# Linear attention feeding a sine-gated MLP on one core: one weight quarter loaded ahead of another, and the second chunk's query turns and scores placed anew

## The chip, the cores and the metric

The kernel runs on one core of a Trainium2 chip. Five engines work side by side: TensorE (PE; its weight loads are shown as PEld), VectorE (DVE), ScalarE (ACT), GpSimd (POOL) and SyncE (SP). Each takes its own instructions strictly in order and waits for others through semaphores. The metric is the device time of one execution in microseconds, as the median of several runs.

## What is computed

The reference has two parts. The first is block-wise linear attention over q, k, v of shape 4 x 8 x 768 x 64 (batch, heads, positions, width) with a decay `lam` for each head, in blocks of 64 positions; the second takes the attention output as 3072 tokens of 512 numbers and runs a two-layer MLP with the "snake" activation.

```python
for b in range(nb):                       # nb = 768 / 64 blocks
    intra = (qb @ kb.T * Dmask) @ vb      # scores inside the block, masked by powers of lam
    inter = (qb * lam_pow) @ kv_state     # what earlier blocks left
    out[:, :, sl] = intra + inter
    kv_state = lam_block * kv_state + (kb * rev_pow).T @ vb
x = out as (3072, 512)
h = x @ w_in                              # 512 -> 2048
g = h + sin(alpha * h)**2 / alpha
y = g @ w_out                             # 2048 -> 512
```

## The kernel before

The 768 positions are cut into six **chunks** of 128 positions (t = 0 to 5), each over all 4 batches and 8 heads, so a chunk is 512 tokens. For each chunk the MLP runs in a **stage** g. Its first layer is `hidden(g, f)` for f = 0 to 15: four matmuls of 128x128 by 128x512 into one PSUM bank (L507), a sine on ACT (L510), a square on ACT (L515) or, for some f of stage 0 (f = 3, 5, 7, 9, 13), on DVE (L523), and then `finish(g, f)` on DVE (L524), which makes the 512 columns of `gall` from both. Its second layer is cut into 16 **units** (m, part): `project(g, m, part)` is four matmuls (L535) that add a quarter of the 2048 hidden features for 128 tokens into a bank; part p reads `w_out_sb[p]`, the p-th quarter of `w_out`. `w_in_sb[i]` is a quarter of `w_in`, needed by f = 4i to 4i + 3.

The order is written out by hand: the schedule is manual, and each engine runs its instructions in the order in which the program states them. Units of stage g wait in a list and `run(n)` takes the next n of them; they are placed between the other work of PE.

Attention of chunk t + 1 is placed within stage t. It is done in two **pairs** of batches, pr 0 (batches 0, 1) and pr 1 (batches 2, 3), in these steps:

- `turn`, `turns_pair`: PE transposes k or q (L320, L338, L340, L341) into a PSUM bank, and ACT or DVE copies them out (L344, L324).
- `scores`: 32 small matmuls of 64x64 (L443) from the turned k and q into two banks; `masks` multiplies them by the decay table on DVE (L450).
- `states`: 32 matmuls of 64x64 (L423); `update` folds them into the running state on DVE (L399, or L403 in four pieces) and casts it on POOL (L392).
- `outputs_first`: 31 matmuls of 64x64 (L457) of queries with the cast states; it ends with a tiny ACT copy (L472) of two turned columns, for which the first matmul of `outputs` waits. `outputs`: one more L457 and 32 matmuls (L482) of masked scores with v. `leave` scales the result on DVE (L489) into `xt`, the input of the next stage's first layer.

Chunk 0 has a form of its own; chunk 1, the second, is placed by hand in the last third of stage 0, from `hidden(0, 10)` on, and between stages 0 and 1. All of the change but the order of two loads is there.

Loads of k, q, v and of the weights are issued by POOL, each a DMA with a cast from fp32 to bf16; the order of issue is the order of the program. The last loads before the first stage are `load_w_in(0)` in two pieces, then 1, 2, 3, and later in the text, with no other instruction of POOL between, `load_w_out(0)`. Behind it POOL makes `kdec` of chunk 0 (L257) and then issues k, q, v of chunk 1.

PSUM has eight banks. `H0` gives the bank of each `hidden(0, f)`. Those that matter here: the turned k and, in the version after, the turned q of pair 1 of chunk 1 use bank 4; `states` and `scores` are given their two banks in the call.

Of the kernel before, what the change touches and what calls it, by code (L numbers as in the profile page):

```python
# [15 lines left out]
def kernel(  # L16
# [41 lines left out]
    def bank(nm, n, dtype=FP32):  # L58
        return psum.tile([P, 512 if dtype is FP32 else 1024], dtype, name=nm, tag=f"b{n}")
# [27 lines left out]
    def load_w_in(i, w0=0, w1=512):  # L87
        w = slice(512 * i + w0, 512 * i + w1)
        nc.gpsimd.dma_start(out=w_in_sb[i][:, :, w0:w1], in_=moe_w_in[:, w].rearrange("(c p) g -> p c g", p=P))  # L89

    def load_w_out(i):
        nc.gpsimd.dma_start(out=w_out_sb[i][:],
                            in_=moe_w_out[i * 512:(i + 1) * 512, :].rearrange("(f p) d -> p f d", p=P))

    def load(t, nm, b0, b1):
        dst, src = NAT[nm]
        to = dst[t][:, b0:b1, :, :].rearrange("p b h e -> p (b h) e")
        by_head = src[b0:b1, :, t * T:(t + 1) * T, :].rearrange("b h p e -> p (b h) e")
        n = H * (b1 - b0)
        if t > 1 and nm != "v" and b0 == 2:  # L100
            nc.gpsimd.dma_start(out=to[:, 0:n - 1, :], in_=by_head[:, 1:n, :])
            nc.gpsimd.dma_start(out=to[:, n - 1:n, :], in_=by_head[:, 0:1, :])
        else:
            nc.gpsimd.dma_start(out=to, in_=by_head)  # L104
# [20 lines left out]
        nc.gpsimd.dma_start(out=vn[0][:, 3, hs, :], in_=v[3, hs, 0:T, :].rearrange("h p e -> p h e"))  # L125
    load_w_in(0, 0, 2 * P)
    load_w_in(0, 2 * P, 512)
    for i in range(1, 4):
        load_w_in(i)

    fill = consts.tile([P, 512], BF16, name="fill")
    nc.vector.memset(fill[:], 1.0)  # L132
# [3 lines left out]
    def spin(n, bk, cols=256):  # L136
        ps = bank("hps", bk)
        for _ in range(n):
            nc.tensor.matmul(out=ps[:, 0:cols], lhsT=fill[:, 0:P], rhs=fill[:, 0:cols], start=True, stop=True)  # L139
# [82 lines left out]
    V, G, A = nc.vector, nc.gpsimd, nc.scalar  # L222
# [4 lines left out]
    def turned_by_one(t, pr):  # L227
        return bool(t) and pr == 1

    def in_turn(t, pr):  # L230
        return t > 1 and pr == 1

    def where(t, pr, n):
        if turned_by_one(t, pr):
            n = (n - 1) % (2 * H)
        return n % 2, n // 2
# [89 lines left out]
    def halves(hd):  # L326
        return slice(hd * D, (hd + 1) * D)

    def turns_pair(t, nm, b, bk, engines):
        src, n = (kn, 0) if nm == "k" else (qn, 1)  # L330
        ps = bank("T_ps", bk, BF16)[:].rearrange("p (u c i) -> p u c i", u=2, c=HP)
        flat = src[t][:, b:b + 2].rearrange("p b h d -> p (b h) d")
        o = int(turned_by_one(t, b // 2) and not in_turn(t, b // 2))
        for u in range(2):
            for hp in range(HP):
                h = u * H + 2 * hp + o
                if h + 2 <= 2 * H:
                    nc.tensor.transpose(out=ps[:, u, hp, :], in_=flat[:, h:h + 2, :], identity=iden[:])  # L338
                else:
                    nc.tensor.transpose(out=ps[LO, u, hp, :], in_=flat[:, h, :], identity=iden[:])  # L340
                    nc.tensor.transpose(out=ps[HI, u, hp, :], in_=flat[:, 0, :], identity=iden[:])  # L341
        for u, eng in enumerate(engines):
            if eng is nc.scalar:
                eng.copy(out=both[t][:, n, b + u, :, :], in_=ps[:, u])  # L344
            else:
                eng.tensor_copy(out=both[t][:, n, b + u, :, :], in_=ps[:, u])
# [25 lines left out]
    def head(tile, t, pr, n):  # L372
        s = (n - 1) % (2 * H) if in_turn(t, pr) else n
        return tile[t][:, 2 * pr + s // H, s % H, :]
# [12 lines left out]
    def decay_state(n, pr):  # L387
        nc.gpsimd.tensor_tensor(out=pair(SD, pr), in0=pair(S_of[n], pr), op=ALU.mult,  # L388
                                in1=L64[:, pr].unsqueeze(1).unsqueeze(3).broadcast_to([P, 2, HP, D]))

    def cast_state(n, pr, dst):
        nc.gpsimd.tensor_copy(out=pair(dst, pr), in_=pair(S_of[n], pr))  # L392
# [18 lines left out]
    def banks_of(kind, t, prs, ns, nm):  # L411
        ns = ns or [AB[2 * pr + n] for pr in prs for n in range(2)]
        for k, n in enumerate(ns):
            att[kind, t, prs[k // 2], k % 2] = bank(nm, n)[:].rearrange("p (u c i) -> p u c i", u=2, c=HP)

    def states(t, prs=BOTH, ns=None):
        banks_of("KV", t, prs, ns, "KV_ps")
        for pr in prs:
            for h0 in range(0, 2 * H, 2):
                for blk in range(2 if t < NT - 1 else 1):  # L420
                    for h in (h0, h0 + 1):
                        half, m = where(t, pr, h)
                        nc.tensor.matmul(out=att["KV", t, pr, blk][halves(half), m // HP, m % HP, :],  # L423
                                         lhsT=head(kdec, t, pr, h)[halves(blk)],
                                         rhs=vn[t][halves(blk), 2 * pr + h // H, h % H, :], start=True, stop=True)
# [9 lines left out]
    def scores(t, prs=BOTH, ns=None):  # L435
        banks_of("F", t, prs, ns, "F_ps")
        for pr in prs:
            for u in range(2):
                for hp in range(HP):
                    for blk in range(2):  # L440
                        for hd in range(2):
                            w = halves(blk)
                            nc.tensor.matmul(out=att["F", t, pr, hd][w, u, hp, :],  # L443
                                             lhsT=KT[t][halves(hd), 2 * pr + u, hp, w],
                                             rhs=QT[t][halves(hd), 2 * pr + u, hp, w], start=True, stop=True)
# [8 lines left out]
    def inter(t, pr, half, m, blk, start):  # L454
        n = (2 * m + half + turned_by_one(t, pr)) % (2 * H)
        u, h = n // H, n % H
        nc.tensor.matmul(out=att["O", t, pr, blk][halves(h % 2), u, h // 2, :],  # L457
                         lhsT=home(t, blk)[halves(half), 2 * pr + m // HP, m % HP, :],
                         rhs=QT[t][halves(half), 2 * pr + m // HP, m % HP, halves(blk)],
                         start=start, stop=False, skip_group_check=True)  # L460

    def outputs_first(t, prs=BOTH, ns=None):
        banks_of("O", t, prs, ns, "O_ps")
        begun = set()
        order = [(pr, half, m, blk) for m in range(2 * HP) for blk in range(2) for pr in prs for half in range(2)]
        for blk in range(2):
            order.remove((prs[0], 0, 0, blk))
        for pr, half, m, blk in order + [(prs[0], 0, 0, 1)]:
            inter(t, pr, half, m, blk, (pr, half, blk) not in begun)
            begun.add((pr, half, blk))  # L470
        seen = QT[t][LO, 2 * prs[0], 0, 0:T:D]
        nc.scalar.copy(out=seen, in_=seen)  # L472
# [145 lines left out]
    outs(0, 3, 4, None, 1)  # L618
    nc.vector.reciprocal(out=r_sb[:], in_=alpha_sb[:])
    spin(3, 3)  # L620
    load_w_out(0)
    decay_k(0, 0, 2)
    decay_k(0, 2, 4)
    mask_table()
# [25 lines left out]
    def run(n):  # L650
        for _ in range(min(n, len(behind))):
            behind.pop(0)()
# [3 lines left out]
    for f in range(NFC):  # L656
        hidden(0, f)
        if f in (1, 10):
            states1(0, f // 10, 2 if f == 10 else 4)
        if f == 10:  # L660
            decay_k(1, 0, 2)
            decay_state(1, 0)
            cast_state(1, 0, home(1, 0))
            load(1, "q", 2, 4)
            load_w_out(2)
            load_w_out(3)
            load(2, "v", 0, 2)
        if f in (11, 12):
            run(1)
        if f == 12:  # L670
            turns_pair(1, "k", 0, 4, (A, A))
        if f == 13:
            turn(1, "q", 0, 2, V)
            turn(1, "q", 1, 3, V)
        if f == 14:
            scores(1, (0,), (4, 2))
            masks(1, 0)
        if f == 15:
            run(1)
            states(1, (0,), (4, 2))  # L680
            finish(0, 14)
            update(1, 0, 0)
        if f != 14:
            finish(0, f)
# [1 line left out]
    decay_state(1, 1)  # L686
    cast_state(1, 1, home(1, 0))
    update(1, 1, 0)
    run(2)
    turns_pair(1, "k", 2, 4, (A, A))  # L690
    run(1)
    outputs_first(1, (0,), (5, 0))
    load(2, "v", 2, 4)
    run(1)
    outputs(1, (0,))
    leave(1, 0)
    states(1, (1,), (4, 2))
    update(1, 0, 1)
    run(1)
    turns_pair(1, "q", 2, 5, (A, A))  # L700
    load(2, "k", 0, 2)
    run(1)
    update(1, 1, 1)
    scores(1, (1,), (5, 0))
    masks(1, 1)
    load(2, "k", 2, 4)
    outputs_first(1, (1,), (4, 2))
    load(2, "q", 0, 2)
    load(2, "q", 2, 4)
    run(2)  # L710
    outputs(1, (1,))
    leave(1, 1)
    run(2)
# [100 lines left out]
```

## Time and profile before

| what | value |
|---|---|
| median of 3 runs | 207.41 us (207.37 to 207.46) |
| the profiled execution's own time | 207.33 us |
| its span, first to last instruction | 205.6 us |
| time around the span | 1.7 us |
| granted TensorE clock, mean | 0.999 |
| PE busy | 198.1 us (96%) |
| DVE, ACT, POOL busy | 131.5, 143.2, 106.5 us (64%, 70%, 52%) |
| L507, first-layer matmuls | 94.3 us |
| L535, second-layer matmuls | 90.4 us |

In a timeline row the columns are: start and length in us from the span's start, engine, line, operation, what it writes and reads with its shape, how many instructions were merged into the row, and in square brackets how long the engine sat idle before it and what ended that. A row of PE gives 1.04 us for four matmuls of 512 columns, yet the next row starts 0.86 us after it: matmuls are pipelined, so the pace is read from start to start. Some matmul records are missing in a trace (a row says x3 where four ran), and then the start of the row is late.

### The profile page before, as it was taken

What the parts mean: (1) busy time and instruction counts of PE and PEld (TensorE: products, weight loads), DVE (VectorE), ACT (ScalarE), POOL (GpSimd) and SP (SyncE); (2) the same over time, 40 slices, a digit from 0 to 9 for tenths busy, and PEclk for the clock granted to TensorE, in tenths of its full rate; (3) what the DMA queues carried; (4) which work ended last, traced back from release to release, by engine and by line L of the source; (5) the groups of instructions that cost most, each with busy time, mean ns of one, the idle gap of its engine ahead of it and who ended that gap; (6) DMA issues with size and microseconds to landing.
All of it is one profiled execution on the core that took longest, in us unless ns stands there. A gap on an engine that the chain in (4) does not pass through costs nothing.

```text
span 205.6 us, 5385 instructions
## 1 busy us (share of the span) xinstructions
PE 198.1 (96%) x2235; PEld 98.3 (48%) x2265; DVE 131.5 (64%) x219; ACT 143.2 (70%) x241; POOL 106.5 (52%) x112
## 2 busy tenths in 40 slices
PE   7999989999999999999999999999999999999994
PEld 2764445554454444445444445444445444444443
DVE  7794979473889878967556967555967544444000
ACT  7798987224999799676776666776666787887121
POOL 8999939988979975999966930002000000000000
PEclk9999999999999999999999999999999999999999
DMA  8999999999989999899999929401101101110213
GB/s 132 170 178 205 203 162 176 189 176 154 150 275 105 128 151 184 82 150 155 152 149 155 181 64 192 117 3 51 54 0 54 51 0 54 53 51 0 104 51 105
DMA packets 96683, 24.49 MB, mean 119 GB/s; under 512 B 87938, under 2 KB 94226, under 8 KB 96658
## 3 DMA queue, kind: packets, MB, share of 16 engines
q0 software_dynamic: 74528, 13.37, 86.9%
q1 hardware_dynamic: 22128, 10.76, 25.5%
q8 instruction: 18, 0.29, 0.6%
q14 instruction: 7, 0.06, 0.1%
q10 hardware_dynamic: 2, 0.00, 0.0%
HBM read 27.27 MB, written 6.29 MB: 163 GB/s over the span
## 4 chain that ended last, share of the span: by engine, by line
PE 84%; DMA 7%; POOL 6%; issue 1%; ACT 1%; POOLq 0%; ACTq 0%
PE ops L535 39%; PE hps L507 35%; DMA w_out<-in_moe_w_out_dram 7%; PE O_ps L457 2%; POOL w_in L89 2%; PE hps L560 2%; PE F_ps L443 2%; PE KV_ps L423 2%; POOL kn L104 1%; PE O_ps L482 1%; POOL vn L104 1%; PE T_ps L338 1%; POOL qn L114 1%; POOL vn L125 1%; ACT QKT L344 1%
## 5 line engine op out<-in xcount | busy, mean ns | idle before, releaser
L524 DVE SCALAR_TENSOR_TENSOR gall<-s,r_sb,hps 128x512 bf16<-128x512 bf16 x96 | 71.1, 745 | 44.5 <-ACT s L515 44.3
L507 PE MATMUL hps<-xt,w_in 128*128 128x512 bf16 x369 | 94.3, 379 | 1.1 <-issue 0.3
L535 PE MATMUL ops<-w_out,gall 128*128 128x512 bf16 x353 | 90.4, 380 | 1.7 <-DMA w_out<-in_moe_w_out_dram 0.6
L510 ACT ACTIVATE s_sb<-hps,alpha_sb 128x512 bf16<-128x512 f32 x96 | 65.2, 684 | 32.0 <-PE hps L507 31.5
L515 ACT ACTIVATE s<-s_sb 128x512 bf16<-128x512 bf16 x91 | 57.3, 630 | 2.8
L507 PEld LDWEIGHTS <-w_in 128*128 128x128 bf16 x384 | 36.6, 98 | 42.8 <-DMA w_in<-in_moe_w_in_dram 0.3
L535 PEld LDWEIGHTS <-gall 128*128 128x128 bf16 x368 | 34.6, 98 | 41.5 <-DMA w_out<-in_moe_w_out_dram 1.1
L257 POOL TENSOR_TENSOR kdec<-kn,R 128x1024 bf16<-128x1024 bf16 x12 | 22.9, 1937 | 4.2 <-DMA kn<-in_k_dram 4.1
L392 POOL CAST sb<-S 128x512 bf16<-128x512 f32 x20 | 12.3, 621 | 21.3 <-DVE S L399 21.3
L388 POOL TENSOR_TENSOR SD<-S,L 128x512 f32<-128x512 f32 x16 | 16.8, 1050 | 8.6 <-DVE S L399 8.5
L489 DVE TENSOR_TENSOR xt<-O_ps,Etab 128x512 bf16<-128x512 f32 x20 | 12.8, 684 | 6.4 <-PE O_ps L482 6.4
L104 POOL DMA_DIRECT2D vn<-in_v_dram x13 | 14.7, 1137 | 0.0
L542 DVE COPY o_sb<-ops 128x512 f32<-128x512 f32 x15 | 10.3, 689 | 4.2 <-PE ops L535 4.2
L450 DVE TENSOR_TENSOR STm<-F_ps,C 128x512 bf16<-128x512 f32 x20 | 12.8, 683 | 0.3 <-PE F_ps L443 0.3
L544 ACT COPY o_sb<-ops 128x512 f32<-128x512 f32 x8 | 4.6, 576 | 12.0 <-PE ops L535 12.0
L399 DVE TENSOR_TENSOR S<-SD,KV_ps 128x512 f32<-128x512 f32 x16 | 10.8, 683 | 0.1
L104 POOL DMA_DIRECT2D kn<-in_k_dram x9 | 10.0, 1113 | 0.4 <-issue 0.3
L344 ACT COPY QKT<-T_ps 128x512 bf16<-128x512 bf16 x8 | 4.3, 586 | 5.3 <-PE T_ps L341 5.3
L139 PE MATMUL hps<-fill 128*128 128x256 bf16 (+1 forms) x24 | 6.5, 391 | 1.4 <-DVE fill L132 1.4
L104 POOL DMA_DIRECT2D qn<-in_q_dram x6 | 7.1, 1188 | 0.0
L457 PEld LDWEIGHTS <-sb 64*64 64x64 bf16 x320 | 4.3, 108 | 4.8 <-issue 4.7
L356 DVE TENSOR_TENSOR STm<-F_ps,C 128x512 bf16<-128x512 f32 x8 | 5.2, 686 | 0.8 <-PE F_ps L352 0.4
(92 smaller groups left out, 116.8 us busy)
## 6 DMA issues: line engine op xcount, KB each, us to landing
out_dram<-o_sb SPq DMA_DIRECT2D x19, 256.0 KB, 2.4
vn<-in_v_dram POOLq DMA_DIRECT2D x10, 256.0 KB, 7.9
w_out<-in_moe_w_out_dram POOLq DMA_DIRECT2D x4, 512.0 KB, 10.8
w_in<-in_moe_w_in_dram POOLq DMA_DIRECT2D x3, 512.0 KB, 9.4
kn<-in_k_dram POOLq DMA_DIRECT2D x6, 256.0 KB, 8.7
qn<-in_q_dram POOLq DMA_DIRECT2D x6, 256.0 KB, 8.5
out_dram<-o_sb SPq DMA_DIRECT2D x8, 128.0 KB, 1.8
kn<-in_k_dram POOLq DMA_DIRECT2D x4, 240.0 KB, 6.7
```

Source lines behind the costliest of these rows:

```text
L104: nc.gpsimd.dma_start(out=to, in_=by_head)
L257: nc.gpsimd.tensor_tensor(out=kdec[t][:, b0:b1, :, :], in0=kn[t][:, b0:b1, :, :], in1=R[:, o:o + H].unsqueeze(1).unsqueeze(3).broadcast_to ...
L388: nc.gpsimd.tensor_tensor(out=pair(SD, pr), in0=pair(S_of[n], pr), op=ALU.mult, in1=L64[:, pr].unsqueeze(1).unsqueeze(3).broadcast_to([P, ...
L392: nc.gpsimd.tensor_copy(out=pair(dst, pr), in_=pair(S_of[n], pr))
L399: nc.vector.tensor_tensor(out=S, in0=pair(SD, pr), in1=ps, op=ALU.add)
L450: nc.vector.tensor_tensor(out=st[:, hd], in0=att["F", t, pr, hd], op=ALU.mult, in1=of_mask(C64, t, pr, hd).unsqueeze(1).broadcast_to([P, 2 ...
L489: nc.vector.tensor_tensor(out=xview(t)[:, 2 * pr:2 * pr + 2, blk, :, :], in0=att["O", t, pr, blk], in1=Eb, op=ALU.mult)
L507: nc.tensor.matmul(out=hps[:], lhsT=w[:, c, (f % 4) * P:(f % 4 + 1) * P], rhs=xt[g][:, c, :], start=(c == 0), stop=(c == NDC - 1))
L510: nc.scalar.activation(out=s_sb[:], in_=hps[:], func=ACTF.Sin, scale=alpha_sb[:, f:f + 1])
L515: nc.scalar.activation(out=s2[:], in_=s_sb[:], func=ACTF.Square)
L524: nc.vector.scalar_tensor_tensor(out=gall[g][:, f, :], in0=s2[:], scalar=r_sb[:, f:f + 1], in1=hps[:], op0=ALU.mult, op1=ALU.add)
L535: nc.tensor.matmul(out=ops[:], lhsT=gall[g][:, f, m * P:(m + 1) * P], rhs=w_out_sb[part][:, f % 4, :], start=(f == 0), stop=(f == NFC - 1))
```

## The change

Three edits. First, `load_w_out(0)` is moved from behind the set-up of chunk 0 to between `load_w_in(2)` and `load_w_in(3)`. As no other POOL instruction stands between the two places, the order of POOL's issues changes by a swap of these two loads alone.

Second, in stage 0 the turns of q of pair 0 move from f = 13 to f = 14, and `scores` and `masks` of pair 0 from f = 14 to f = 15. On PE `hidden(0, 14)` now stands before the turns of q and `hidden(0, 15)` before the scores. On DVE the two copies of the turned q (L324) stand behind the square and the `finish` of f = 13, where they stood ahead of them.

Third, behind stage 0: three units instead of two run before the turns of k of pair 1, and none between these turns and `outputs_first` of pair 0. The turns of q of pair 1 move ahead of `states` of pair 1, into bank 4 instead of 5. `states` of pair 1 writes banks 2 and 4 instead of 4 and 2, and `scores` of pair 1 follows it at once; the two units that stood between `states` and `outputs_first` stand now between `scores` and `outputs_first`, one unit runs between the turns of q and `states`, and one instead of two between `outputs_first` and `outputs` of pair 1. No instruction is added or removed on any engine; the number of units run up to the start of stage 1 is the same (the line numbers of the changed kernel are two higher behind the first edit, one of them taken back at the second).

```diff
     load_w_in(0, 2 * P, 512)
-    for i in range(1, 4):
-        load_w_in(i)
+    load_w_in(1)
+    load_w_in(2)
+    load_w_out(0)
+    load_w_in(3)
...
     spin(3, 3)
-    load_w_out(0)
     decay_k(0, 0, 2)
...
         if f == 12:
             turns_pair(1, "k", 0, 4, (A, A))
-        if f == 13:
+        if f == 14:
             turn(1, "q", 0, 2, V)
             turn(1, "q", 1, 3, V)
-        if f == 14:
+        if f == 15:
             scores(1, (0,), (4, 2))
             masks(1, 0)
-        if f == 15:
             run(1)
             states(1, (0,), (4, 2))
             finish(0, 14)
...
     update(1, 1, 0)
-    run(2)
+    run(3)
     turns_pair(1, "k", 2, 4, (A, A))
-    run(1)
     outputs_first(1, (0,), (5, 0))
     load(2, "v", 2, 4)
     run(1)
     outputs(1, (0,))
     leave(1, 0)
-    states(1, (1,), (4, 2))
+    turns_pair(1, "q", 2, 4, (A, A))
+    run(1)
+    states(1, (1,), (2, 4))
     update(1, 0, 1)
-    run(1)
-    turns_pair(1, "q", 2, 5, (A, A))
     load(2, "k", 0, 2)
+    scores(1, (1,), (5, 0))
     run(1)
     update(1, 1, 1)
-    scores(1, (1,), (5, 0))
     masks(1, 1)
     load(2, "k", 2, 4)
+    run(1)
     outputs_first(1, (1,), (4, 2))
     load(2, "q", 0, 2)
     load(2, "q", 2, 4)
-    run(2)
+    run(1)
     outputs(1, (1,))
```

## The prediction

> **What bounds the kernel now.** I read the page first: TensorE is busy nearly throughout and nearly all of the chain that ended last is TensorE's, with one foreign piece of size, a weight load.
>
> ```profile
> span 205.6 us, 5385 instructions
> PE 198.1 (96%) x2235; PEld 98.3 (48%) x2265; DVE 131.5 (64%) x219; ACT 143.2 (70%) x241; POOL 106.5 (52%) x112
> PE 84%; DMA 7%; POOL 6%; issue 1%; ACT 1%; POOLq 0%; ACTq 0%
> ```
>
> Next I asked for TensorE's waits from 48 us to the end. One group is left:
>
> ```profile
> PE hps L507 <- issue: 0.3, 2, 0.2
> ```
>
> From stage 1 on TensorE waits for nobody, so what the change is worth is the shift of the first matmul of stage 1, `hidden(1, 0)`, and the rest of the program follows it. The timeline of TensorE has the stretch where the second chunk is placed in stage 0:
>
> ```profile
> 25.61 1.04 PE L507 MATMUL hps<-xt,w_in 128*128 128x512 bf16 x4
> 27.28 1.04 PE L535 MATMUL ops<-w_out,gall 128*128 128x512 bf16 x4 [0.63 <-DMA w_out<-in_moe_w_out_dram]
> 28.15 1.03 PE L507 MATMUL hps<-xt,w_in 128*128 128x512 bf16 x4
> ...
> 29.88 0.61 PE L338 MATMUL T_ps<-iden,kn 128*128 128x128 bf16 x8
> 30.33 1.03 PE L507 MATMUL hps<-xt,w_in 128*128 128x512 bf16 x3
> 31.19 0.61 PE L320 MATMUL T_ps<-iden,qn 128*128 128x128 bf16 x8
> 31.64 1.03 PE L507 MATMUL hps<-xt,w_in 128*128 128x512 bf16 x4
> 32.59 0.45 PE L443 MATMUL F_ps<-QKT 64*64 64x64 bf16 x32
> 32.97 0.82 PE L507 MATMUL hps<-xt,w_in 128*128 128x512 bf16 x3
> 33.84 1.03 PE L535 MATMUL ops<-w_out,gall 128*128 128x512 bf16 x4
> ```
>
> From start to start, four wide matmuls take 0.865 us (28.15 to 29.88 is two groups), a set of eight turns 0.45 us (29.88 to 30.33), four wide ones ahead of a 64x64 set 0.95 us (31.64 to 32.59), the set itself 0.38 us. `hidden(0, 11)` starts at 25.61, so its successor, unit (0, 0), could start at 26.47; it starts at 27.28. The wait is 0.81 us, for `w_out`'s first quarter.
>
> **Edit 1, the two loads.** The loads' rows:
>
> ```profile
> 13.50 13.73 DMA w_out<-in_moe_w_out_dram
> L89 POOL DMA_DIRECT2D w_in<-in_moe_w_in_dram x5: 812/826/842, 9.8 to 12.8; - x5
> DMA to landing us min/median/max: 5.2/7.6/11.2
> ```
>
> The fifth and last `w_in` piece is issued at 12.8 and lands, being the slowest, after 11.2 us, at 24.0. `w_out` lands at 13.50 + 13.73 = 27.23, the next in line. The two have the same size and adjacent issues, so I let them trade places: `w_out` lands near 24.0 and unit (0, 0) runs at 26.47, which gains 0.81. `w_in`'s last quarter is first read by `hidden(0, 12)`, at 26.47 + 0.865 = 27.34; if it lands at 27.23, it is in time by 0.1. The last place took 3.2 us, from 24.0 to 27.2. If that length goes with the place or with the load, the sum of both is the same and 27.23 stands. If the load behind `w_out`'s is slow and `w_out` as well, `w_in` lands 0.6 later at about 27.85 (the piece before lands at 12.0 + 9.4, 2.6 ahead of 24.0, by the same view). I take 27.23.
>
> The turns of k then run at 27.34 + 1.73 = 29.07. Their k had landed when POOL's `kdec` started on it:
>
> ```profile
> 28.95 1.90 POOL L257 TENSOR_TENSOR kdec<-kn,R 128x1024 bf16<-128x1024 bf16 x1 [3.16 <-DMA kn<-in_k_dram]
> ```
>
> So they come through with 0.1 to spare, for the loads behind the swapped pair keep their places.
>
> **Edit 2, turns of q and scores one f later.** Laid out by the steps above: `hidden(0, 13)` 29.52, `hidden(0, 14)` 30.38, turns of q 31.24 (their q was there by 31.19 in the version before), `hidden(0, 15)` 31.69, scores 32.64, unit (2, 0) 33.02. That is 0.82 ahead of 33.84, if the scores find their q. ACT and DVE decide that:
>
> ```profile
> 27.99 0.63 ACT L515 ACTIVATE s<-s_sb 128x512 bf16<-128x512 bf16 x1
> 29.22 0.69 ACT L510 ACTIVATE s_sb<-hps,alpha_sb 128x512 bf16<-128x512 f32 x1 [0.60 <-PE hps L507]
> 30.53 1.07 ACT L344 COPY QKT<-T_ps 128x512 bf16<-128x512 bf16 x2
> 31.49 0.70 ACT L510 ACTIVATE s_sb<-hps,alpha_sb 128x512 bf16<-128x512 f32 x1
> 31.61 0.76 DVE L324 COPY QKT<-T_ps 128x512 bf16<-128x512 bf16 x2 [0.27 <-PE T_ps L320]
> 32.33 0.42 DVE L523 TENSOR_TENSOR s<-s_sb 128x512 bf16<-128x512 bf16 x1
> 32.79 0.75 DVE L524 SCALAR_TENSOR_TENSOR gall<-s,r_sb,hps 128x512 bf16<-128x512 bf16 x1
> 33.45 1.28 DVE L450 TENSOR_TENSOR STm<-F_ps,C 128x512 bf16<-128x512 f32 x2
> ```
>
> Before, the sine of f = 12 waited for TensorE. Now `hidden(0, 12)` is 0.81 earlier, and the sine would be ready at 28.41 (29.22 - 0.81), but ACT is in the square of f = 11 until 28.62; operations overlap by some 0.1, so it starts at 28.53, which is 0.69 earlier than before. From there ACT is the chain: square, two copies of turned k, then the sine of f = 13, 2.27 behind the first sine as before, at 30.80, with its end at 31.50.
>
> DVE's order is what the edit turns round. Before, the copies of turned q (31.61) stood ahead of the square (32.33) and `finish` (32.79) of f = 13; now they stand behind. The square starts at 31.53, `finish` 0.46 later at 31.99, the copies 0.66 later (32.79 to 33.45) at 32.65, ending at 33.41. The first half of the scores needs the first copy only, the second half the second, and starts at 33.46; half a set is 0.24 to the next start. Unit (2, 0) starts at 33.70, not 33.02: the scores wait 0.68. **Of the 0.81 there are 0.14 left at unit (2, 0)** (33.84 - 33.70). The bounds: no wait of the scores keeps 0.82, and a first half that waits as well for both copies puts unit (2, 0) at 33.84, gain nothing. I take 0.14, as each matmul waits for what it reads. Behind the copies, `masks` start some 0.3 later than before, and the state updates of pair 0 with them; unit (1, 1), put ahead of the turns, covers them, since the first outputs come not before 38.2.
>
> **Edit 3, the units dealt anew.** The stretch to stage 1:
>
> ```profile
> 36.91 0.55 PE L338 MATMUL T_ps<-iden,kn 128*128 128x128 bf16 x7
> 38.55 0.69 PE L457 MATMUL O_ps<-QKT,sb 64*64 64x64 bf16 x31
> 39.17 1.04 PE L535 MATMUL ops<-w_out,gall 128*128 128x512 bf16 x4
> 40.14 0.46 PE L482 MATMUL O_ps<-STm,vn 64*64 64x64 bf16 x32
> 40.41 0.49 PE L423 MATMUL KV_ps<-vn,kdec 64*64 64x64 bf16 x32
> 41.71 0.55 PE L338 MATMUL T_ps<-iden,qn 128*128 128x128 bf16 x7
> 42.48 1.07 ACT L344 COPY QKT<-T_ps 128x512 bf16<-128x512 bf16 x2 [3.00 <-PE T_ps L341]
> 43.60 0.45 PE L443 MATMUL F_ps<-QKT 64*64 64x64 bf16 x32 [0.20 <-ACT QKT L344]
> 43.88 0.67 PE L457 MATMUL O_ps<-QKT,sb 64*64 64x64 bf16 x31
> ...
> 48.45 1.89 PE L507 MATMUL hps<-xt,w_in 128*128 128x512 bf16 x7
> ```
>
> TensorE's work is the same; what differs is where wide and 64x64 work meet, and one wait.
> - *Meetings.* Each entry into a 64x64 set costs 0.09 (0.95 against 0.865). Behind unit (2, 0) there were five: states, first outputs, outputs with states, scores with first outputs, outputs. Now there are six: the states leave the outputs, the scores join the states, the first outputs stand alone. Cost 0.09.
> - *Turns of k straight before first outputs.* Not in the trace. Turns plus unit plus entry took 1.64 (36.91 to 38.55), so the turns 0.69 with the unit and entry taken off; if this meeting needs no entry it saves 0.09, if it needs one it is neutral against the count above. I take 0.05 saved. The Trainium skill, TensorEngine Tiling (Array Packing), Key Properties, says that a change of tiling mode drains the array; by it this meeting pays, and the sum below is 0.05 higher. For wide matmuls ahead of 64x64 ones the trace agrees with its 0.09; no row shows this meeting.
> - *The wait.* Before, scores started 1.89 behind the turns of q (41.71 to 43.60), held by ACT's two copies; turns, one unit and entry are 0.66 + 0.95 = 1.61, so 0.28 was lost. Now one unit stands between the turns and the states, and the states' second bank is the turns' bank 4, which ACT must have copied out: again 1.89 against 1.61. The wait moves from scores to states and keeps its size. At best it goes (-0.28), at worst the DVE work behind it comes late: states and scores now run together, and first outputs need bank 4 back from the state update. Two wide units (1.73) cover that work; I take nothing, with 0 to 0.15 as bounds.
>
> **The sum.** 0.14 gained at unit (2, 0), 0.09 lost, 0.05 saved: 0.10 us, `hidden(1, 0)` at 48.35 instead of 48.45. DMA loads of chunk 2 are issued up to 0.7 later by POOL but queue behind earlier ones, so I cost that at nothing. The profiled execution took 207.33 with its span of 205.6, so 207.23 for such a one; the median shown, 207.41, is 0.08 above, so I forecast **207.3**. A measurement of this kernel can tell about 0.2% (0.41 us) from no change; 0.10 is inside.
>
> **The rivals** (times as medians, so with the 0.08).
> - *Faster, the wait at the scores mostly stays away* (18%): everything of edit 1 is kept but edit 3's 0.04, 0.77 in all, 206.6; with half of the wait, 207.0. For it: the square of f = 13 is only just later than the old slot of the copies. Against: DVE's order is fixed and the sine of f = 13 cannot pass ACT's two copies of k, all with durations from rows.
> - *Slower, `w_in`'s last quarter comes late* (27%): it lands at 27.85 and on. The point from which it decides is 27.34. At 27.85, `hidden(0, 12)` starts 0.55 later, its sine at 28.97 instead of 28.53, and everything in the chain of ACT and DVE with it: 0.44 lost, of which 0.10 was gained, 207.75; a landing another 0.5 us later gives 208.2. For it: spare time is 0.1 us, and the load in the last place took 0.6 longer than the others. Against: nothing in DMA order but the swap changes. A hold-up of first outputs or outputs of pair 1 behind DVE would add 0.15 to either.
> - *The swap does not do what it says*: if the wait only changes its name, `hidden(0, 12)` waits in place of unit (0, 0), some 0.8 behind 27.34; that is the upper end of the rival before, 208.0 to 208.2, and within its 27% I give it a quarter.
>
> **Numbers.** The forecast, no change, 55%: its own range 206.95 to 207.7. Faster 18%, slower 27%. The range that holds 8 in 10 reaches from 206.7 to 208.0.
>
> **What would show it.** In the changed profile: no wait at the first `w_out` matmul, which starts near 26.5; `hidden(0, 12)` near 27.35 without a wait for `w_in`; DVE's copies of turned q near 32.65, behind `finish`, and scores of pair 0 waiting for them, unit (2, 0) near 33.7; states of pair 1 starting 1.9 behind the turns of q; `hidden(1, 0)` near 48.35, and no wait after it. A wait of `hidden(0, 12)` for `w_in` makes the second rival true; copies of q before 32.3 make the first.

## The result and the profile after

| | before | after |
|---|---|---|
| median of 11 runs each | 207.55 us | 209.19 us |
| lowest and highest | 207.27 to 209.10 | 208.42 to 210.08 |
| profiled execution, own time | 207.33 us | 209.50 us |
| its span | 205.6 us | 207.6 us |

The ratio after to before is 1.0068, with a 95% interval from 1.0050 to 1.0086: the change makes the kernel slower, by 1.4 us by this ratio (the two medians lie 1.6 apart). One run before took 209.10; the other ten lie between 207.27 and 208.01, so the runs after spread wider. A run over 1.5% above the fastest of its kernel counts as slow and is left out of ratios and ranges here; in all the sets below only two are (210.62 and 210.78 of f1). The forecast was 207.3, no change, with a range of 206.7 to 208.0. The measured time lies outside it on the slower side, but the sign of the slower rival, a wait of `hidden(0, 12)` for `w_in`, is not in the profile.

The page of the changed kernel, lines of busy time and of the chain by engine:

```profile
span 207.6 us, 5385 instructions
PE 197.9 (95%) x2236; PEld 97.6 (47%) x2265; DVE 131.7 (63%) x219; ACT 142.9 (69%) x241; POOL 106.9 (51%) x112
PE 73%; DMA 8%; ACT 7%; POOL 6%; issue 3%; DVE 3%; ACTq 0%; DVEq 0%; POOLq 0%
```

TensorE is busy for as long as before (197.9 against 198.1) in a span that is 2.0 longer, and in the chain it has given 11 of its 84 hundredths to ACT, DVE, issue and DMA. No engine's busy time moved by more than 0.4; TensorE waits more. Its five longest waits between 14 and 70 us (who waited, for what, us in total, times, longest):

```profile
PE T_ps L340 <- DMA qn<-in_q_dram: 0.8, 1, 0.8
PE ops L537 <- issue: 0.5, 3, 0.2
PE F_ps L445 <- DVE QKT L326: 0.4, 1, 0.4
PE hps L509 <- DMA w_in<-in_moe_w_in_dram: 0.4, 1, 0.4
PE KV_ps L425 <- DVE STm L452: 0.3, 1, 0.3
```

The wait for `w_out` is gone, as the change meant. There are four others: turns of q in stage 1 for their load, scores for DVE's copies, states for the masks, and the very first use of `w_in` (there TensorE's weight load waited 0.7; in the version before it waited 0.3 and the matmuls did not). The row `issue` stands with the same 0.5 in the version before. The timeline of TensorE, with the rows that answer to those of before:

```profile
26.41 1.04 PE L509 MATMUL hps<-xt,w_in 128*128 128x512 bf16 x4
27.28 1.03 PE L537 MATMUL ops<-w_out,gall 128*128 128x512 bf16 x4
28.14 1.03 PE L509 MATMUL hps<-xt,w_in 128*128 128x512 bf16 x4
...
32.05 0.61 PE L322 MATMUL T_ps<-iden,qn 128*128 128x128 bf16 x8
32.49 1.03 PE L509 MATMUL hps<-xt,w_in 128*128 128x512 bf16 x4
33.94 0.56 PE L445 MATMUL F_ps<-QKT 64*64 64x64 bf16 x32 [0.42 <-DVE QKT L326]
34.43 0.55 PEld L537 LDWEIGHTS <-gall 128*128 128x128 bf16 x4
34.66 0.81 PE L537 MATMUL ops<-w_out,gall 128*128 128x512 bf16 x3 [0.16 <-issue]
35.40 0.22 PE L425 MATMUL KV_ps<-vn,kdec 64*64 64x64 bf16 x2
35.96 0.44 PE L425 MATMUL KV_ps<-vn,kdec 64*64 64x64 bf16 x30 [0.34 <-DVE STm L452]
36.33 2.76 PE L537 MATMUL ops<-w_out,gall 128*128 128x512 bf16 x12
...
44.13 1.90 PE L537 MATMUL ops<-w_out,gall 128*128 128x512 bf16 x7
46.11 0.66 PE L459 MATMUL O_ps<-QKT,sb 64*64 64x64 bf16 x31
...
49.81 1.89 PE L509 MATMUL hps<-xt,w_in 128*128 128x512 bf16 x8
...
60.16 0.68 PE L340 MATMUL T_ps<-iden,qn 128*128 128x128 bf16 x8 [0.77 <-DMA qn<-in_q_dram]
```

Read from start to start between the same pieces of work (unit (2, 0) by its weight load at 34.43, since its first matmul has no record), the two traces differ like this:

| stretch | before | after | difference | forecast |
|---|---|---|---|---|
| start to `hidden(0, 11)` | 25.61 | 26.41 | +0.80 | 0 |
| to unit (0, 0) | 1.67 | 0.87 | -0.80 | -0.81 |
| to unit (2, 0), with turns of q and scores | 6.56 | 7.15 | +0.59 | +0.67 |
| to unit (3, 0), with states of pair 0 | 1.34 | 1.90 | +0.56 | 0 |
| to `hidden(1, 0)` | 13.27 | 13.48 | +0.21 | +0.04 |
| to the turns of q in stage 1 | 9.40 | 10.35 | +0.95 | 0 |
| to the end | 147.7 | 147.4 | -0.3 | 0 |

The two rows that I did foresee came out within 0.1. The first row cancels the gain of the second in this pair of traces: the first piece of `w_in` landed 6.1 us after its issue here and 5.2 there, stage 0 began late, and so TensorE reached unit (0, 0) at the very 27.28 at which it got `w_out` before. The rows with +0.56 and +0.95 were not in the forecast at all. Two views tell where they come from. DVE:

```profile
32.72 0.75 DVE L526 SCALAR_TENSOR_TENSOR gall<-s,r_sb,hps 128x512 bf16<-128x512 bf16 x1
33.38 0.75 DVE L326 COPY QKT<-T_ps 128x512 bf16<-128x512 bf16 x2
34.61 1.29 DVE L452 TENSOR_TENSOR STm<-F_ps,C 128x512 bf16<-128x512 f32 x2 [0.48 <-PE F_ps L445]
```

The masks run from 34.61 to 35.90. Scores and states of pair 0 use the same two PSUM banks, 4 and 2, so the states cannot write them until the masks have read them: two states matmuls start at 35.40, the other thirty at 35.96, behind the masks. In the kernel before, the states come here:

```profile
34.80 0.45 PE L423 MATMUL KV_ps<-vn,kdec 64*64 64x64 bf16 x32
```

There the masks ended at 33.45 + 1.28 = 34.73, so the states were in time by 0.07. `hidden(0, 15)`, which the change puts ahead of the scores, had been the work that covered the masks. POOL's queue has the other cause:

```profile
44.78 0.61 POOL L394 CAST sb<-S 128x512 bf16<-128x512 f32 x1 [1.78 <-DVE S L401]
45.48 1.15 POOL L104 DMA_DIRECT2D kn<-in_k_dram  x1
46.62 0.62 POOL L394 CAST sb<-S 128x512 bf16<-128x512 f32 x1
47.18 1.20 POOL L101 DMA_DIRECT2D kn<-in_k_dram  x1
48.37 0.59 POOL L102 DMA_DIRECT2D kn<-in_k_dram  x1
48.95 1.17 POOL L104 DMA_DIRECT2D qn<-in_q_dram  x1
50.09 1.22 POOL L101 DMA_DIRECT2D qn<-in_q_dram  x1
```

The loads of chunk 2 stand in POOL's order behind a cast of the state, which waits for DVE, which waits for the states of pair 1 on TensorE. These start at 43.22, where the kernel before has them at 40.41, and DVE's update at 44.02 instead of 41.86. That makes the cast, and with it all loads of k and q behind it, 2.2 us late: the first q load is issued at 48.95, where the kernel before has

```profile
42.61 0.61 POOL L392 CAST sb<-S 128x512 bf16<-128x512 f32 x1 [0.69 <-DVE S L399]
...
46.78 1.17 POOL L104 DMA_DIRECT2D qn<-in_q_dram  x1
```

The load issued at 50.09 takes 10.0 us to land (60.1), where those of before took 6.2 to 7.1 us. TensorE comes for it near 59.3 and waits.

### The profile page after: what moved, and what is told of

Same layout as the page of the kernel before. It is cut to its first block, busy times and chain, and to the rows that moved or that the text cites. A ratio compares the mean times of both kernels' runs of the same rounds, so it can differ in the third digit from the quotient of the medians.

```text
span 207.6 us, 5385 instructions
## 1 busy us (share of the span) xinstructions
PE 197.9 (95%) x2236; PEld 97.6 (47%) x2265; DVE 131.7 (63%) x219; ACT 142.9 (69%) x241; POOL 106.9 (51%) x112
## 4 chain that ended last, share of the span: by engine, by line
PE 73%; DMA 8%; ACT 7%; POOL 6%; issue 3%; DVE 3%; ACTq 0%; DVEq 0%; POOLq 0%
PE ops L537 33%; PE hps L509 31%; DMA qn<-in_q_dram 5%; ACT s_sb L512 4%; DMA w_in<-in_moe_w_in_dram 3%; PE O_ps L459 2%; ACT s L517 2%; PE hps L562 2%; PE F_ps L445 2%; PE KV_ps L425 1%; POOL kn L104 1%; POOL vn L104 1%; PE O_ps L484 1%; ACT QKT L346 1%; DVE STm L452 1%
## 5 line engine op out<-in xcount | busy, mean ns | idle before, releaser
L491 DVE TENSOR_TENSOR xt<-O_ps,Etab 128x512 bf16<-128x512 f32 x20 | 12.8, 684 | 5.9 <-PE O_ps L484 5.9
L452 DVE TENSOR_TENSOR STm<-F_ps,C 128x512 bf16<-128x512 f32 x20 | 12.8, 682 | 0.5 <-PE F_ps L445 0.5
```

Of the source, the lines that this page charges most:

```text
L452: nc.vector.tensor_tensor(out=st[:, hd], in0=att["F", t, pr, hd], op=ALU.mult, in1=of_mask(C64, t, pr, hd).unsqueeze(1).broadcast_to([P, 2 ...
L491: nc.vector.tensor_tensor(out=xview(t)[:, 2 * pr:2 * pr + 2, blk, :, :], in0=att["O", t, pr, blk], in1=Eb, op=ALU.mult)
```

## The experiments

Theory A: the loss is made by the order of the second chunk. Rival B: the swap of the two loads disturbs the loads from the start, as the late first weight suggests. Times are medians; each set was timed beside the kernel before, whose median was 207.66 in the first two sets, 207.79 in the third and 207.68 in the last.

### The kernel before once more, and each half of the change alone

No edit.

> The kernel before, unchanged, for a trace beside the others of this set. Theory A (the loss is made by the order of the second chunk, behind 27 us): the first w_in piece can land as late here as in the changed kernel's trace (15.95 against 15.04 us), and the lateness is swallowed at unit (0, 0), which waits for w_out until 27.2 to 27.4 either way; hidden(1, 0) near 48.5. Rival B (the swap of the loads disturbs the loads from the start): the first w_in piece lands near 15.0 here, and 0.9 later in every kernel with the swap.

One run took 207.36. The first `w_in` piece landed after 5.1 us, `hidden(0, 11)` started at 26.14, unit (0, 0) at 27.25, `hidden(1, 0)` at 48.46. The start was 0.5 later than in the first trace of this same kernel (26.14 against 25.61) and `hidden(1, 0)` at the same place: what is late ahead of unit (0, 0) disappears in its wait for `w_out`. The first piece of `w_in` was not late at all, against theory A's guess; TensorE had waited 0.4 for loads of q of chunk 0 instead.

```diff
-    for i in range(1, 4):
-        load_w_in(i)
+    load_w_in(1)
+    load_w_in(2)
+    load_w_out(0)
+    load_w_in(3)
...
-    load_w_out(0)
     decay_k(0, 0, 2)
```

> Edit 1 alone: the two loads trade places, the order of the second chunk stays as before. Theory A: not slower; unit (0, 0) no longer waits, and the gain is what TensorE is early by then, between 0 (first w_in piece late) and 0.5 us (the turns of q, in their old place, then wait for q, which lands near 30.7): 207.0 to 207.5. Rival B: this alone is 0.8 to 1.5 us slower than before.

207.56, ratio 0.9992 (0.9974 to 1.0009): no difference that can be told. That ends rival B, which asked for 0.8 us or more. In its trace unit (0, 0) starts at 27.02 without a wait, 0.23 earlier than in c1, and `hidden(1, 0)` at 48.53, 0.07 later: the stretch between takes 21.51 us against 21.21. The next loads are in the way; these two rows of TensorE's weight loads (which wait longer than the matmuls behind them) are the waits for k and q of chunk 1:

```profile
PEld L340 <- DMA kn<-in_k_dram: 0.6, 2, 0.4
PEld L322 <- DMA qn<-in_q_dram: 0.5, 1, 0.5
```

The third variant is the changed kernel with the swap undone (edits 2 and 3 as they are):

```diff
-    load_w_in(1)
-    load_w_in(2)
-    load_w_out(0)
-    load_w_in(3)
+    for i in range(1, 4):
+        load_w_in(i)
...
+    load_w_out(0)
     decay_k(0, 0, 2)
```

> Edits 2 and 3 without edit 1: the loads in their old order. Theory A: slower than before by 1.4 to 2.1 us (states of pair 0 wait 0.5 for the masks, scores wait 0.5, the q loads of chunk 2 are issued 2 us later and the turns of q in stage 1 wait 0.8 for them), so 209.0 to 209.6. Rival B: within 0.3 us of before.

209.51, ratio 1.0086 (1.0054 to 1.0118), as theory A has it: the whole loss is there without the swap (the interval overlaps that of the changed kernel). The trace has both waits of the second chunk, about as long as in the changed kernel:

```profile
PE F_ps L443 <- DVE QKT L324: 0.5, 1, 0.5
PE KV_ps L423 <- DVE STm L450: 0.3, 1, 0.3
```

It does not have the third, which theory A expected as well: q was issued at 48.90 and landed after 8.2 to 9.2 us, and its turns started 0.08 late. The profiled run took 208.65, close to the fastest of the ten (208.61). So what makes the median 0.9 us longer than this run is in no trace of c3.

### Edit 2 and edit 3, each alone on the kernel before

```diff
-        if f == 13:
+        if f == 14:
             turn(1, "q", 0, 2, V)
             turn(1, "q", 1, 3, V)
-        if f == 14:
+        if f == 15:
             scores(1, (0,), (4, 2))
             masks(1, 0)
-        if f == 15:
             run(1)
```

> Edit 2 alone on the kernel before: turns of q of pair 0 at f = 14, scores and masks at f = 15. Theory A1 (the larger part of the loss is edit 2's): in the trace scores of pair 0 wait 0.5 to 0.7 for DVE's copies and states of pair 0 wait about 0.55 for the masks, which read the same banks; hidden(1, 0) 1.0 to 1.1 late, near 49.5; 208.4 to 208.9. Rival A2 (edit 3's new order makes most of it): hidden(1, 0) late by less than 0.5.

208.47, ratio 1.0045 (1.0028 to 1.0062). `hidden(1, 0)` starts at 49.60 instead of 48.46, and its rows show where:

```profile
33.95 0.56 PE L443 MATMUL F_ps<-QKT 64*64 64x64 bf16 x32 [0.60 <-DVE QKT L324]
...
35.96 0.44 PE L423 MATMUL KV_ps<-vn,kdec 64*64 64x64 bf16 x30 [0.34 <-DVE STm L450]
36.33 1.90 PE L535 MATMUL ops<-w_out,gall 128*128 128x512 bf16 x8
...
49.60 1.89 PE L507 MATMUL hps<-xt,w_in 128*128 128x512 bf16 x7
```

From unit (0, 0) at 27.10 to unit (3, 0) at 36.33 are 9.23 us, against 7.94 (27.25 to 35.19) in c1: 1.29 lost by the two waits, and from there to `hidden(1, 0)` 13.27 as before. Theory A1 holds, with `hidden(1, 0)` 1.14 late. The q loads were issued 1.15 later (47.93), and no turn waited for them.

Edit 3 alone is the third hunk of the diff shown above, from `run(3)` on.

> Edit 3 alone on the kernel before. Theory A1: hidden(1, 0) 0.2 to 0.3 late (one more entry into 64x64 work, first outputs of pair 1 behind the state update), and the q loads of chunk 2 issued 0.8 to 1.3 later than before, so that turns of q in stage 1 wait between 0 and 0.8: 207.6 to 208.5. Rival A2: hidden(1, 0) over 0.8 late and over 208.5.

208.09, ratio 1.0023 (1.0010 to 1.0037). `w_out` landed late in the profiled run, so I count from unit (0, 0): 27.82 to `hidden(1, 0)` at 49.20 is 21.38, against 21.21 in c1, 0.17 lost; from there to the turns of q in stage 1 (58.84) 9.64 against 9.40, 0.24 lost. The q loads were issued at 48.3, 1.5 later than before; 0.5 of this is the late `w_out`, and 1.0 is edit 3's own order, which puts the turns of q and a unit ahead of the states of pair 1. So edit 3 costs little at its own place and something through the loads. The two alone add up to 0.68% and both together without the swap cost 0.86%; the intervals allow the sum.

### Taking single waits out of the changed kernel

First the loads of chunk 2: those of k and q are issued ahead of the last state cast.

```diff
     load(2, "k", 0, 2)
+    load(2, "k", 2, 4)
+    load(2, "q", 0, 2)
+    load(2, "q", 2, 4)
     scores(1, (1,), (5, 0))
...
-    load(2, "k", 2, 4)
     run(1)
     outputs_first(1, (1,), (4, 2))
-    load(2, "q", 0, 2)
-    load(2, "q", 2, 4)
```

> The changed kernel, but POOL issues the last loads of k and those of q of chunk 2 right behind the first load of k, ahead of the state cast of pair 1 that waits for DVE. Theory A: the turns of q in stage 1 no longer wait for q (0.8 us in the changed kernel's trace), so 0.6 to 0.9 us faster than the changed kernel, about 208.2. Rival B: no faster than the changed kernel by more than 0.2 us.

208.67, ratio 1.0040 (1.0025 to 1.0055), where the changed kernel has 1.0068; and its twelve runs lie between 208.47 and 208.81, where the changed kernel's eleven lie between 208.42 and 210.08. In the trace q is issued 0.5 earlier (48.44), and from `hidden(1, 0)` to its turns are 9.65 us, 0.25 over the 9.40 of before, where the changed kernel has 0.95 over. The two kernels were timed in different sets and their intervals overlap a little, so that the late loads of k and q cost half a microsecond in the median is likely and not settled; the narrower spread is plain. A little less than expected was won: the first cast of pair 1 still stands ahead of these loads, and q is still issued 1.7 later than before.

Next, with these early loads kept, states of pair 0 one unit later.

```diff
-            run(1)
+            run(2)
             states(1, (0,), (4, 2))
...
-    run(3)
+    run(2)
     turns_pair(1, "k", 2, 4, (A, A))
```

> The changed kernel with the early q loads of c4, and states of pair 0 one unit later (two units run between scores and states, two instead of three ahead of the turns of k). Theory A1: the wait of states for the masks goes (0.56), hidden(1, 0) near 49.3 instead of 49.88, 208.0 to 208.3 against 208.67. Rival A3 (the wait moves on, to first outputs of pair 0, which need the state cast): within 0.2 of 208.67.

208.33, ratio 1.0040 (1.0016 to 1.0064): by the ratio nothing is won against c4, and by its width nothing can be told. The trace shows that the wait for the masks is gone, and from `hidden(0, 12)` to `hidden(1, 0)` it takes 21.44 (28.12 to 49.56) where c4 takes 21.95 (27.93 to 49.88): 0.51 of the 0.56 arrives there. The turns of q in stage 1 then wait 0.27 for their load (49.56 to 59.23 is 9.67 against 9.40). The mechanism is shown, its worth in time is not.

Then, from c4 again, DVE's copies of q ahead of the square and `finish` of f = 13.

```diff
         if f == 14:
             turn(1, "q", 0, 2, V)
             turn(1, "q", 1, 3, V)
+            finish(0, 13)
...
-        if f != 14:
+        if f not in (13, 14):
             finish(0, f)
```

> The changed kernel with the early q loads of c4, and on DVE the two copies of turned q ahead of the square and finish of f = 13. Theory A1: scores of pair 0 no longer wait for the copies (0.5 to 0.7 in c3 and c4) and masks come as much earlier, hidden(1, 0) near 49.2, 208.0 to 208.2 against 208.67. Rival A3 (scores are held by ACT's copies of k or by q's landing, not by DVE's order): within 0.2 of 208.67.

208.17, ratio 1.0021 (0.9995 to 1.0046), not to be told from c4 by the intervals. The copies run at 31.99 and the scores follow `hidden(0, 15)` at 32.97 with no wait, so it was DVE's order that held them. But a new wait appears at once:

```profile
32.97 0.45 PE L445 MATMUL F_ps<-QKT 64*64 64x64 bf16 x32
33.98 1.02 PE L537 MATMUL ops<-w_out,gall 128*128 128x512 bf16 x3 [0.56 <-DVE gall L526]
34.93 0.68 PE L425 MATMUL KV_ps<-vn,kdec 64*64 64x64 bf16 x32
```

Unit (2, 0) adds up in bank 1, which `hidden(0, 13)` used, and waits for `finish` of f = 13, now behind the copies. The states' wait for the masks shrinks meanwhile, as the masks come earlier, and from `hidden(0, 12)` to `hidden(1, 0)` 0.56 is won against c4 (21.39).

### Does the late q load do it alone?

```diff
+    scratch = consts.tile([P, B, HP, D], FP32, name="scratch")
+    for _ in range(2):
+        nc.gpsimd.tensor_tensor(out=pair(scratch, 0), in0=pair(SD, 0), in1=pair(SD, 0), op=ALU.mult)
     load(2, "q", 0, 2)
     load(2, "q", 2, 4)
     run(2)
     outputs(1, (1,))
```

> The kernel before with two idle multiplications on POOL (about 1.05 us each, into a tile that nobody reads) ahead of the q loads of chunk 2, which so are issued at 48.9 instead of 46.8, as late as in the changed kernel; nothing else moves. Theory (the late issue alone makes the q wait of stage 1 and its spread): hidden(1, 0) stays at 48.46, the turns of q in stage 1 start up to 1.5 late, 207.9 to 208.8, with a wider spread than the kernel before. Rival (the wait needs the later hidden(1, 0) or other moved loads as well): within 0.2 of the kernel before.

207.95 (207.72 without 210.62 and 210.78), ratio 1.0010 (0.9985 to 1.0034): inconclusive in time, and with these two left out nearer to the rival. In the profiled run q was issued at 49.09 and landed after 4.9 to 7.6 us, and no turn waited. Ten of its runs reach from 207.33 to 209.59, those of the kernel before beside it from 207.27 to 208.93, too little apart to call a wider spread shown. So a late issue of q alone is not shown to cost anything, and by its trace it need not. Two things differ from the changed kernel. The loads of k went out at 43.5 to 46.4 here, as before, and only q was late; in the changed kernel k goes out at 45.5 to 48.4, right ahead of q. And `hidden(1, 0)`, behind which the turns come, is 1.2 earlier here. That k and q late together make the long landing fits, and no run tests it. SyncE's DMA transposes, which run beside these loads from near 50.5 on in both, do not do it alone: the q loads of f1 ran beside them as well.

### One more wait covered in the kernel before

Besides the one for `w_out` the kernel before has one wait in this stretch: scores of pair 1 behind ACT's copies, 0.28. Two units instead of one cover it:

```diff
     turns_pair(1, "q", 2, 5, (A, A))
     load(2, "k", 0, 2)
-    run(1)
+    run(2)
     update(1, 1, 1)
...
     load(2, "q", 2, 4)
-    run(2)
+    run(1)
     outputs(1, (1,))
```

> The kernel before with two units instead of one between the turns of q of pair 1 and their scores, and one instead of two before the outputs of pair 1. If the 0.28 us that scores lose behind ACT's two copies is a plain wait, two units (1.73) cover it: no wait there, hidden(1, 0) near 48.2 instead of 48.46, 207.3 to 207.45 against 207.66. Rival: the masks then end after TensorE reaches the outputs of pair 1, and hidden(1, 0) stays within 0.1.

207.32 against 207.79, ratio 0.9984 (0.9969 to 0.9998): by the ratio 0.3 us faster, and the interval only just leaves out no change. The trace:

```profile
42.33 0.55 PE L338 MATMUL T_ps<-iden,qn 128*128 128x128 bf16 x7
...
42.99 1.90 PE L535 MATMUL ops<-w_out,gall 128*128 128x512 bf16 x8
44.82 0.45 PE L443 MATMUL F_ps<-QKT 64*64 64x64 bf16 x32
...
48.80 1.24 PE L507 MATMUL hps<-xt,w_in 128*128 128x512 bf16 x5
```

The scores start 1.83 behind the start of the two units, with no wait, and from the turns of q to `hidden(1, 0)` are 6.47 us, against 6.74 (41.71 to 48.45) before: 0.27 of the 0.28. The rival did not happen, by little: the masks end at 46.61, and the outputs start at 46.66. That `hidden(1, 0)` stands at 48.80 is due to `w_out`, which landed 14.4 us after its issue in this run. The same with the swap:

> The same with the two loads traded (edit 1). If the swap's gain is cut by the landing of later loads (k and q of chunk 1), as in c2, this stays within 0.2 of e1. Rival: with the wait at the scores gone, the swap's gain shows: 0.3 to 0.8 faster than e1.

207.37, ratio 0.9982 (0.9963 to 1.0001), the same as e1: no gain of the swap is to be seen.

## Why the prediction was wrong, step by step

- **Edit 1, the two loads trade places**: right. In the changed kernel `w_out` landed 12.0 us after its issue at 12.8, and `hidden(0, 12)` followed unit (0, 0) without a wait for `w_in`. TensorE was 0.8 later there than the prediction had it, so that `w_in` was in time is partly luck. In the twelve traces that give it, the last of the two landed at 26.7 to 27.9 whichever it was.
- **"which gains 0.81"**: the wait went, its worth was mis-sized. 0.81 was the wait of one execution with an early start; in c1 TensorE reached the place 0.5 later (0.4 of it for loads of q of chunk 0), in the changed kernel's trace 0.8 later (the first `w_in` piece). That piece landed 5.5 to 6.1 us after its issue in the six traces with the swap and 5.1 to 5.8 in the seven without; the ranges overlap, and a small effect of the swap on it is neither shown nor ruled out. The wait for `w_out` had absorbed what came late before it. Without it the loads of k and q of chunk 1 set the pace: in c2 they took back the 0.23 that unit (0, 0) was early. The prediction's "0.1 to spare" for k came from one trace too: POOL's `kdec`, which waits for k, starts at 28.95 there and at 29.05 to 29.57 in the twelve others. The swap alone has ratio 0.9992; by its interval it gains at most 0.3%.
- **Edit 2, "the scores wait 0.68"**: right in mechanism and size. The stretch is 0.59 longer where 0.67 was forecast; d4 shows that DVE's order makes it. The forecast set it against a gain of 0.81 that did not come, so in the time it is a loss.
- **"Behind the copies, `masks` start some 0.3 later ... unit (1, 1) ... covers them"**: this is the step that failed first in the order of the kernel. I looked for who waits for the state updates and for the first outputs, and not for who waits for the masks' banks. `states` writes banks 4 and 2, which `masks` reads; there were two pieces of 0.865 between scores and states before, with 0.07 to spare, and the change leaves one. Price 0.56 in the changed kernel, c3, c4 and d1, gone in d3.
- **"DMA loads of chunk 2 are issued up to 0.7 later by POOL ... I cost that at nothing"**: the second failure. They were issued 2.2 later. They stand behind a state cast, so each wait of TensorE upstream is passed on to them (1.15 in d1, by edit 2 alone), and edit 3's own order adds 1.0 (d2), more than the 0.7 by itself. Cost 0.95 in the profiled run; in c4, with 0.5 of earlier issue, the median is half a microsecond lower (across sets). The cost is not a fixed one: with q issued at 48.1 to 49.1 the turns started 0 late in f1, 0.08 in c3, about 0.25 in c4, d2 and d3, and 0.95 in the changed kernel. Why the landing differs so stays open.
- **Edit 3, meetings of wide and 64x64 work**: 0.04 forecast, 0.21 measured. The first outputs start 0.66 behind the turns of k (38.93 to 39.59), as a wide unit does behind the turns of q in the kernel before (41.71 to 42.37), so this meeting shows no entry of its own. The Trainium skill, TensorEngine Tiling (Array Packing), Key Properties, says that a change of tiling mode drains the array. By it I had set 0.05 more as the other bound, and the measured 0.66 decides against that bound here. It does not show that a change is free: the last of these turns is split in two rows of another shape (128*64), so the shape changes in both cases. First outputs of pair 1 start 1.98 behind their two units (44.13 to 46.11), 0.15 over the 1.83 of such a stretch. That fits a wait for bank 4, which I had with 0 to 0.15 as bounds: DVE's update, which reads it, ends at 45.97 (44.85 + 1.12). No row names this wait, so it is not shown.
- **The wait that "moves from scores to states and keeps its size"**: right in mechanism, and a little smaller. Two matmuls of the states start 1.64 behind the turns of q (41.58 to 43.22), with no wait. The other thirty start at 43.48, just behind ACT's copies, which run from 42.36 for 1.08 and free bank 4; that is 1.90 behind the turns, where 1.89 was forecast. As two were under way by then, the next unit starts 2.55 behind the turns (44.13), where the forecast and two sets of 0.38 would have it 2.65 behind.
- **The rivals**: in the changed kernel's trace neither happened. In c4 and d4, where TensorE came earlier, `hidden(0, 12)` did wait for `w_in`, by about 0.1. The slower side came from mechanisms that I had not listed, so 27% for slower was too little.
- **The sum**: a gain of 0.10 was forecast, and the pair of traces lost 2.0. Of the 2.1 between them, 0.80 is edit 1's gain, which the late start took back, 0.56 the masks, 0.95 the late loads and 0.17 edit 3; 0.08 at the scores and 0.3 behind stage 1 go the other way. The median is 1.6 longer, so this pair is somewhat worse than the usual run.

## What to carry to other kernels

When work is moved ahead of a producer, list every consumer of every buffer that the producer's chain holds, PSUM banks above all, and ask how much cover each had: a trace shows a cover of 0.07 us as no wait at all. Then follow the delay into the queues of other engines; loads that stand in program order behind a computed result are late whenever that result is. And a wait that is large in one profile may be the place where lateness from upstream is absorbed, which differs from run to run: take it away and the next load in line can set the same pace.

## What was not expected of the hardware

The same first load landed 5.1 to 6.1 us after its issue from run to run, and the last of the early weight loads at 26.7 to 27.9. Loads of q issued 2 us later landed once 4.9 to 7.6 us (f1) and once 8.8 to 10.0 us (the changed kernel) after their issue, so the landing of a load at this place is no fixed offset from its issue.

The last row of the table, -0.3, is mostly one set of matmuls: the first outputs of chunk 2 took 0.90 us from start to next start before (65.25 to 66.15) and 0.64 after (67.58 to 68.22). TensorE's records name no wait there, but DVE's rows point to one. The first two rows are the kernel before, the last two the changed kernel:

```profile
64.16 1.28 DVE L450 TENSOR_TENSOR STm<-F_ps,C 128x512 bf16<-128x512 f32 x2
65.25 0.91 PE L457 MATMUL O_ps<-QKT,sb 64*64 64x64 bf16 x63
...
65.74 1.28 DVE L452 TENSOR_TENSOR STm<-F_ps,C 128x512 bf16<-128x512 f32 x2
67.58 0.71 PE L459 MATMUL O_ps<-QKT,sb 64*64 64x64 bf16 x63
```

In this chunk scores and outputs use the same four banks, so the first outputs cannot write a bank until the masks have read it. In the nine traces in which the masks end inside the set, 0.16 to 0.2 behind its start, the set takes 0.87 to 0.91; in the other four (the changed kernel, c4, d2 and d3), where they have ended before it starts, 0.64 to 0.70. So it is the same kind of wait as that of the states of pair 0, and in the changed kernel, whose q came so late, 0.26 of the lateness is given back there.
